# Attention block with a routed path: the first eleven stretches in another written order, and tanh, gate and product of the routed path at other places

## The chip, the cores and the metric

The kernel runs on one core of one Trainium2 chip. A core has five engines that work side by side, each through its own instructions in the order in which the program gives them: TensorE (PE, with its weight loads shown as PEld), VectorE (DVE), ScalarE (ACT), GpSimd (POOL) and SyncE (SP), which here only issues DMA transfers. An engine that waits for another one is told so by a semaphore, and what stands behind the waiting instruction on that engine waits too. The metric is the device time of one execution in microseconds (us), the median over several runs.

## The reference

The computation has two paths over the same 2048 rows of 640 features. `xn` is the layer norm of `x`.

```python
xn = layernorm(x)                                  # 2048 x 640
q  = xn @ wq                                       # 32 heads of 192
k, v = last 512 rows of the caches, per head
s  = concat_heads(softmax(q @ k.T * 192**-0.5) @ v) @ wo
r  = xn @ w_r                                      # routed path: the two rows with the largest r
y  = (silu(x_sel @ w_gate) * (x_sel @ w_up)) @ w_down * sigmoid(r_sel)
g  = silu(xn + scatter of y to those two rows)
out = x + s * g
```

Nearly all the arithmetic is in the first path: the query projection, the scores, the weighted values and the output projection.

## The kernel before

**Units, steps and stretches.** A unit is 128 query rows of one pair of heads; there are 256. A step is four units (512 rows, one pair of heads), and its query projection is three groups of five matmuls, one group for each 128 of the pair's 384 columns. Units are worked in 86 stretches: stretches 0 and 1 have two units each, all others three (unit n of 4 or more is in stretch 2 + (n-4)//3). What is done for a unit is spread over several stretches: its scores in one, its weighted values in the next, its share of the output projection some stretches later.

**Everything has a written place.** The program is emitted with a manual schedule: each engine's order is the order of the statements. Stretches 11 to 84 come from a function that writes the same order for each (`stretch`), the last from a list, and the first eleven (0 to 10, which also hold the layer norm and the first loads) from a list of tokens, `FIRST`, one line for each stretch after the opening line. A token is an operation and its numbers:

- `x.t.lo.hi` loads rows of x (SP's queue; `.a` at the end: ACT's queue); `k`, `v`, `wq`, `wo` load the other operands; `kT.p` transposes the keys of pair p by DMA on SP.
- `bn`, `as` take the layer norm's sums (on DVE, or on ACT with a short tail on POOL); `sq`, `rc`, `pw` form the scale; `ap.n.e` applies it to row block n on engine e (v DVE, a ACT, g POOL); `turn` and `xT` transpose the result, on PE or by DMA on SP.
- `q.i.c` is the projection group c of step i on PE, `qe` takes it out of PSUM, scaled (a `v` at the end: DVE; otherwise ACT, so also where numbers stand behind the letter, as in all of step 0, which is done in halves).
- `S.j` are the scores of stretch j on PE; `M.n.h` is the row maximum of unit n, head h on DVE; `E.n.h` the exponential on ACT; `P.n` the DMA transpose of the result on SP.
- `O.n` or `OO.n.m` are the weighted values on PE, `Oe` takes them out, divided by the sums (`R`, DVE); `T.j` is their DMA transpose; `W.w` is one block of the output projection on PE, `We` takes it out.
- `sx` and `ex` are tiny activations that bring in the tables of the square root and of the exponential; `B.j.s` runs what the rest of the program has put down for stretch j, slot s. Nothing is put down for a stretch before the twelfth, so the `B` tokens of the list issue nothing.

**PSUM.** Two banks (`ps_f`) serve the projection groups, single `O.n` and the transposes on PE; six (`ps_p`) serve the scores, `OO` and the output projection. A new tile gets the bank whose last reader stands earliest in the written order, and PE waits until that reader is done. The three groups of a step therefore need the first group to be out before the third can start.

**The routed path** rides in the slots of the stretches: `at(n, slot, f)` puts f into the stretch of unit n. In a stretch written by the function, slot 0 is directly behind the scores' matmuls, slot 1 behind the last exponential and its transpose, slot 2 behind the first output projection block and its way out, slot 3 at the very end. `m_mul` is a small gate-and-up product for 512 of 1536 columns (20 matmuls, a tanh, two operations on DVE, then `m_hT`, a DMA transpose). `m_tanh(n)` and `m_gate(n)` (ACT L627, DVE L630) turn row block n into the silu factor; the tanh's target is one of two buffers, by n even or odd, so a tanh must wait for the gate of two blocks before. The step from a stretch to the next on DVE is: values out, transposed, what stands in slot 3, then the next stretch's row maxima.

Of the kernel before, what the change touches and what calls it, by code (L numbers as in the profile page):

```python
# [21 lines left out]
def kernel(ctx, tc, A_x, A_k_cache, A_v_cache, A_wq, A_wo, B_x, B_w_r, B_w_gate, B_w_up, B_w_down, out):  # L22
    nc = tc.nc
    P = 128
    _, S, D = A_x.shape
# [3 lines left out]
    W = min(4096, max(256, Sk // 4))  # L29
# [45 lines left out]
    def f_tile(shape, dtype, name):  # L75
        return ps_f.tile(shape, dtype, name=name, tag="f")
# [358 lines left out]
    M = {}  # L435
# [119 lines left out]
    def m_ffn_piece(fb, q):  # L555
        def f():
            if q == 0:
                M["wgu"] = M["w"].tile([P, 2, DC, 512], BF16, name="wgu", tag="w")
            w, dc = divmod(q, DC)
            src = (B_w_gate, B_w_up)[w].rearrange("(c p) f -> p c f", p=P)  # L560
            nc.sync.dma_start(out=M["wgu"][:, w, dc, :], in_=src[:, dc, fb * 512:(fb + 1) * 512])
        return f

    def m_mul(fb):
        def f():
            gu = f_tile([P, 2, P], FP32, "gu_ps")
# [49 lines left out]
    def m_add(n):  # L616
        def f():
            nc.gpsimd.tensor_scalar(out=xn[:, n, :], in0=xn[:, n, :], scalar1=0.5, scalar2=0.0, op0=ALU.mult, op1=ALU.add)
            for j in range(2):
                yh = M["s"].tile([P, D], BF16, name="yh", tag="t1")  # L620
                nc.gpsimd.tensor_scalar(out=yh, in0=M["y_bc"][:, j, :], scalar1=M["oh"][:, n, j:j + 1], scalar2=0.0, op0=ALU.mult, op1=ALU.add)  # L621
                nc.gpsimd.tensor_tensor(out=xn[:, n, :], in0=xn[:, n, :], in1=yh, op=ALU.add)  # L622
        return f

    def m_tanh(n):
        M["z", n] = M["ws"[n % 2]].tile([P, D], FP32, name="tz", tag=("w", "t2")[n % 2])
        nc.scalar.activation(out=M["z", n], in_=xn[:, n, :], func=ACT.Tanh)  # L627

    def m_gate(n):
        nc.vector.scalar_tensor_tensor(out=xn[:, n, :], in0=M["z", n], scalar=1.0, in1=xn[:, n, :], op0=ALU.add, op1=ALU.mult)  # L630
# [128 lines left out]
    for fb, n0 in enumerate((72, 91, 106)):  # L759
        for q in range(2 * DC):  # L760
            at(n0 + q, 0, m_ffn_piece(fb, q))
        at(n0 + 14, 2, m_mul(fb))
        at(n0 + 14, 3, m_hT(fb))
    for q in range(FC // 2):
        at(121 + 2 * q, 0, m_wd_piece(q))
    at(124, 3, m_sig)
    at(138, 2, m_down)
    for n in range(NTB):
        at(147 + 2 * n, 3, m_add(n))
        at(186 + 2 * n, 1, lambda n=n: m_tanh(n))  # L770
        at(186 + 2 * n, 3, lambda n=n: m_gate(n))
    at(220, 3, fin_open)


# [5 lines left out]
    for j in range(2, NST):  # L780
        due = sum(st_of[4 * i] <= j + 1 for i, _ in todo)
        k = max(due, 2) if j % 4 != 1 else max(due, 3)
# [3 lines left out]
        k = 2 if len(ready) >= 2 and len(q_in[j]) <= 2 and (done + 1) <= 1.5 * (j - 4) else 1  # L786
        k = {NST - 4: 1, NST - 3: 1, NST - 2: 3, NST - 1: 2}.get(j, k)
# [69 lines left out]

    for token in FIRST:
# [43 lines left out]
```

## Time and profile before

| | |
|---|---|
| runs | 803.88 us median of 3 (802.24 to 804.67) |
| profiled execution | 803.23 us, span 801.5 us, granted TensorE clock 0.996 |
| busy in the span | PE 785.5, DVE 625.2, ACT 482.0, POOL 174.8 us |
| first 120 us | PE busy 111.6 us |
| 300 to 400 us | PE busy 100.0 us |
| last 61.5 us | PE busy 54.7 us |

The profile is of one execution. A row of the timeline gives the start in us from the span's first instruction, the time from the first start to the last end, the engine (SPq is SP's queue issuing a DMA), the line, the operation, output and inputs, and how many instructions are merged; in brackets stands idle time before it and what ended that. In the rows by windows the figures are, for each stretch of time, busy us of PE, PEld, DVE, ACT and POOL with their counts, the granted TensorE clock (1.00 is full), the DMA engines' mean share and GB/s. Durations of neighbours overlap: two exponentials that last 0.67 us each with a readout behind them start 0.66 us apart, so a step in a chain is taken from start to start.

### The profile page before, as it was taken

The page shows a single profiled execution, that of the slowest core. Times are in us where ns is not written, and L with a number is a line of the kernel's source. Part 1 is how long each engine was busy: PE and PEld are TensorE (multiplying, and loading weights), DVE is VectorE, ACT ScalarE, POOL GpSimd, SP SyncE. Part 2 cuts the span into 40 slices and gives each one's busy share as a digit, 9 for nine tenths or more (in the row PEclk, how much of TensorE's full clock was granted, in tenths as well). Part 3 has the DMA queues.
Part 4 walks back from the last instruction along what each step waited for, and adds up shares of the span by engine and source line. Part 5 has one row for each costly group of instructions (what it writes and reads, how often), then busy time and mean ns, then how long its engine had stood idle before and what let it go on. Part 6 is the DMA issues. An engine that isn't in the chain of part 4 may idle for free. (4 is left out here: it accounts for less than half of the span.)

```text
span 801.5 us, 15649 instructions
## 1 busy us (share of the span) xinstructions
PE 785.5 (98%) x5748; PEld 481.5 (60%) x5748; DVE 625.2 (78%) x1243; ACT 482.0 (60%) x1303; POOL 174.8 (22%) x194
## 2 busy tenths in 40 slices
PE   8899999999999999999999999999999999999996
PEld 4456556665666566666556665666566665566565
DVE  6876668989888777777777777777788887877786
ACT  7886676556655556655565556565566865565560
POOL 1330000000000000000001999920000000265954
PEclk9999999999999999999999999999999999999999
DMA  8999998789979999699997999879997889997994
GB/s 239 192 207 218 201 189 143 136 183 193 177 137 201 205 206 206 128 216 199 215 219 139 164 188 201 143 140 173 201 165 137 160 177 202 168 195 154 166 176 117
DMA packets 453389, 143.80 MB, mean 179 GB/s; under 512 B 422350, under 2 KB 452816, under 8 KB 453312
## 3 DMA queue, kind: packets, MB, share of 16 engines
q1 hardware_dynamic: 449872, 138.76, 92.8%
q0 software_dynamic: 928, 2.50, 1.1%
q10 hardware_dynamic: 2512, 1.54, 0.7%
q8 instruction: 45, 0.74, 0.4%
q14 instruction: 32, 0.26, 0.1%
HBM read 39.98 MB, written 2.62 MB: 53 GB/s over the span
## 5 line engine op out<-in xcount | busy, mean ns | idle before, releaser
L337 ACT ACTIVATE pexp<-sc,nm 128x512 bf16<-128x512 f32 x512 | 348.4, 696 | 292.5 <-issue 242.5
L330 DVE TENSOR_REDUCE nm<-sc 128x1 f32<-128x512 f32 x512 | 314.7, 681 | 78.7 <-PE sc L322 78.7
L301 PE MATMUL q_ps<-xnT,wq_p 128*128 128x512 bf16 (+1 forms) x975 | 226.3, 376 | 3.2 <-ACT pexp L337 0.8
L404 PE MATMUL w_ps<-wo_g,oT 128*128 128x320 bf16 x1542 | 223.2, 299 | 0.5 <-DMA oT<-o_sb 0.5
L404 PEld LDWEIGHTS <-oT 128*128 128x128 bf16 x1542 | 150.2, 98 | 71.0 <-DMA oT<-o_sb 0.8
L356 PE MATMUL o_ps<-v_sb,pT 128*128 128x192 bf16 x2048 | 185.2, 246 | 2.4 <-DMA pT<-pexp 1.3
L356 PEld LDWEIGHTS <-pT 128*128 128x128 bf16 x2048 | 170.9, 98 | 18.1 <-issue 4.9
L301 PEld LDWEIGHTS <-wq_p 128*128 128x128 bf16 x975 | 88.4, 98 | 127.1 <-issue 37.5
L371 DVE TENSOR_TENSOR o_sb<-o_ps,lsum 128x384 bf16<-128x384 f32 x239 | 131.6, 557 | 40.2 <-PE o_ps L356 22.0
L315 PE MATMUL sc<-kT,qT 128*128 128x512 bf16 x512 | 126.1, 382 | 0.9 <-DMA kT<-k_raw 0.9
L418 DVE TENSOR_TENSOR s_acc<-s_acc,w_ps 128x320 f32<-128x320 f32 x192 | 92.1, 483 | 32.2 <-PE w_ps L404 32.2
L337 ACT ACTIVATION_READ_ACCUMULATOR pexp<-sc,nm 128x1 f32 x512 | 109.8, 214 | 0.0
L293 ACT ACTIVATE qT<-q_ps 128x512 bf16<-128x512 f32 (+1 forms) x179 | 98.8, 606 | 1.3 <-PE q_ps L301 1.1
L315 PEld LDWEIGHTS <-qT 128*128 128x128 bf16 x512 | 49.0, 98 | 42.7 <-issue 2.1
L322 PE MATMUL sc<-kT,qT 64*128 64x512 bf16 x512 | 70.6, 382 | 0.0
L643 POOL TENSOR_TENSOR s_acc<-s_acc,xn 128x640 f32<-128x640 f32 x16 | 22.5, 1403 | 113.7 <-DVE s_acc L418 113.7
L322 PEld LDWEIGHTS <-qT 64*128 64x128 bf16 x512 | 18.1, 94 | 47.0 <-issue 36.8
L622 POOL TENSOR_TENSOR xn<-xn,yh 128x640 bf16<-128x640 bf16 x32 | 44.7, 1396 | 2.7
L612 POOL DMA_DIRECT2D y_d<-y_sb x4 | 2.2, 552 | 172.2 <-DVE y_sb L609 172.2
L644 POOL TENSOR_TENSOR s_acc<-s_acc,x_fin 128x640 f32<-128x640 f32 x16 | 22.4, 1400 | 62.5 <-DMA x_fin<-in_A_x_dram 61.5
L489 POOL DMA_DIRECT2D c_d<-cand x1 | 0.5, 547 | 155.4 <-DVE cand L487 155.4
L621 POOL TENSOR_SCALAR yh<-y_bc,oh 128x640 bf16<-128x640 bf16 x32 | 25.7, 803 | 5.0 <-DMA y_bc<-y_d 3.5
(105 smaller groups left out, 235.2 us busy)
## 6 DMA issues: line engine op xcount, KB each, us to landing
wo_g<-in_A_wo_dram SPq DMA_DIRECT2D x16, 480.0 KB, 4.4
wq_p<-in_A_wq_dram SPq DMA_DIRECT2D x14, 480.0 KB, 5.0
v_sb<-in_A_v_cache_dram SPq DMA_DIRECT2D x16, 384.0 KB, 4.0
k_raw<-in_A_k_cache_dram SPq DMA_DIRECT2D x30, 192.0 KB, 3.2
pT<-pexp SPq DMA_TRANSPOSE x256, 3.7
x_fin<-in_A_x_dram SPq DMA_DIRECT2D x16, 160.0 KB, 2.8
x_in<-in_A_x_dram SPq DMA_DIRECT2D x6, 320.0 KB, 4.8
wgu<-in_B_w_gate_dram SPq DMA_DIRECT2D x15, 128.0 KB, 2.8
```

Of the source, the lines that this page charges most:

```text
L293: nc.scalar.activation(out=out, in_=in_, func=ACT.Copy, scale=scale)
L301: nc.tensor.matmul(q_ps, lhsT=wq_of[g * PAIRS + pr][:, dc, c * P:(c + 1) * P], rhs=xnT[:, t5 * 4 + lo:t5 * 4 + hi, dc, :], start=(dc == 0) ...
L315: nc.tensor.matmul(sc_of[n][hh], lhsT=qT_of[i][:, 2 * hh, u * P:(u + 1) * P], rhs=kp[:, :, 2 * hh, :], start=True, stop=False)
L322: nc.tensor.matmul(sc_of[n][hh], lhsT=qT_of[i][hs, 1, u * P:(u + 1) * P], rhs=kp[hs, :, 1, :], start=False, stop=True)
L330: nc.vector.tensor_reduce(out=nm_of[j][:, c:c + 1], in_=sc_of[n][hh], axis=AX.X, op=ALU.max, negate=True)
L337: nc.scalar.activation(out=pe_of[n][:, hh, :], in_=sc_of[n][hh], func=ACT.Exp, bias=nm_of[j][:, c:c + 1], scale=1.0, accum_out=l_of[j][:, ...
L356: nc.tensor.matmul(ps[:, hh, :], lhsT=pT_of[n][:, hh, jj, :], rhs=v_sb[:, hh, jj, :], start=(jj == 0), stop=(jj == NJ - 1))
L371: nc.vector.tensor_tensor(out=osb_of[j][:, m], in0=ps, in1=l_of[j][:, 2 * m:2 * m + 2].unsqueeze(2).to_broadcast([P, 2, Dh]), op=ALU.mult)
L404: nc.tensor.matmul(w_ps, lhsT=oT_of[j][:, stretches[j].index(n), c % 3, :], rhs=wo_of[g][:, c, lo:hi], start=(c == 0), stop=(c == CPG - 1))
L418: nc.vector.tensor_tensor(out=acc, in0=acc, in1=w_ps, op=ALU.add)
L621: nc.gpsimd.tensor_scalar(out=yh, in0=M["y_bc"][:, j, :], scalar1=M["oh"][:, n, j:j + 1], scalar2=0.0, op0=ALU.mult, op1=ALU.add)
L622: nc.gpsimd.tensor_tensor(out=xn[:, n, :], in0=xn[:, n, :], in1=yh, op=ALU.add)
```

## The change

The list of the first eleven stretches is written in another order, with the same matmuls, scores and transfers. What differs beyond order: two row blocks (4 and 14) take their layer-norm sums on DVE instead of ACT; some ways out of PSUM and applications of the norm change engine; the loads `k.1.0`, `wq.1` and `wq.2` go from ACT's queue to SP's, the loads `x.0.3`, `k.2.1` and `k.3.0` to ACT's; the exponential's table comes in stretch 0 instead of ahead of it.

In the routed path the product for the first 512 columns moves from stretch 29, slot 2 to stretch 30, slot 3, the two others from slot 2 to slot 3 of their stretches (35 and 40). The tanh moves from slot 1 to slot 0, and the gate of an even block from slot 3 to slot 2; the gate of an odd block stays in slot 3.

```diff
     for fb, n0 in enumerate((72, 91, 106)):
         for q in range(2 * DC):
             at(n0 + q, 0, m_ffn_piece(fb, q))
-        at(n0 + 14, 2, m_mul(fb))
-        at(n0 + 14, 3, m_hT(fb))
+        at(n0 + (16, 14, 14)[fb], 3, m_mul(fb))
+        at(n0 + (16, 14, 14)[fb], 3, m_hT(fb))
...
         at(147 + 2 * n, 3, m_add(n))
-        at(186 + 2 * n, 1, lambda n=n: m_tanh(n))
-        at(186 + 2 * n, 3, lambda n=n: m_gate(n))
+        at(186 + 2 * n, 0, lambda n=n: m_tanh(n))
+        at(186 + 2 * n, 2 + n % 2, lambda n=n: m_gate(n))
...
     FIRST = """
-B.3.3 x.0.0.1.a x.0.1.2 k.0.0 bn.0.0 k.0.1.a bn.1.0 x.0.2.3 bn.0.1 sx sq.0.1 wq.0 bn.1.1 sq.1.2 kt.0.a rc.0.1 ap.0.v rc.1.2 kt.1.v x.0.3.4 ap.1.v bn.2.0 turn.0.a turn.1.v q.0.0.0.2 q.0.2.0.2 ex bn.2.1 qe.0.0.v.0.2 k.1.0.a bn.3.0 bn.3.1 qe.0.2.v.0.2 wq.1.a x.1.2.4 q.0.1.0.2 qe.0.1.a.0.2 x.1.0.2 pw.2.4 
-S.0 k.1.1 as.4 ap.2.v ap.3.v turn.2.v turn.3.a M.0.0 q.0.0.2.4 E.0.0 M.1.0 q.0.2.2.4 qe.0.0.v.2.4 E.1.0 bn.7.0 q.0.1.2.4 M.0.1 qe.0.2.v.2.4 v.1 qe.0.1.a.2.4 bn.6.0 B.2.0 bn.7.1 E.0.1 
-S.1 bn.6.1 x.2.0.2 M.1.1 q.1.2 x.2.2.4 as.5 q.1.0 pw.4.8 v.0 M.2.1 E.1.1 qe.1.2.a M.2.0 E.2.0 R.0 M.3.1 E.2.1 as.8 q.1.1 ap.6.g ap.4.v ap.5.v M.3.0 B.3.2 E.3.0 qe.1.0.v P.0 kT.1 bn.11.0 B.3.1 bn.9.0 ap.7.v O.0 qe.1.1.v E.3.1 bn.11.1 P.1 
-S.2 B.3.0 P.2 B.2.1 bn.9.1 xT.4.6 xT.6.8 M.4.0 as.10 P.3 B.4.0 M.5.0 pw.8.12 Oe.0.a M.4.1 O.1 E.5.0 M.5.1 q.2.0 E.5.1 x.3.0.2 Oe.1.v E.4.0 M.6.0 E.6.0 qe.2.0.v T.0 x.3.2.4 E.4.1 P.4 q.2.1 R.1 q.2.2 M.6.1 qe.2.1.v B.2.2 ap.8.g qe.2.2.v E.6.1 ap.9.g O.2 
-S.3 Oe.2.a ap.11.v M.7.0 P.5 M.8.0 M.8.1 as.12 ap.10.g O.3 E.7.0 Oe.3.a P.6 E.8.0 q.3.1 q.3.0 M.9.1 M.9.0 E.8.1 M.7.1 bn.13.0 E.7.1 qe.3.0.v OO.4.5 xT.8.10 R.2 E.9.0 Oe.4.v E.9.1 xT.10.12 qe.3.1.a Oe.5.v q.3.2 qe.3.2.v bn.13.1 P.8 
-S.4 T.1 O.6 as.15 B.2.3 q.4.1 B.7.2 P.7 Oe.6.a M.10.1 P.9 R.3 M.10.0 E.10.0 M.12.0 q.4.0 E.12.0 wo.0.0 M.11.0 wo.0.1 E.10.1 E.11.0 P.10 qe.4.1.v T.2 M.12.1 OO.7.8 M.11.1 E.12.1 qe.4.0.v E.11.1 O.9 Oe.7.v Oe.8.v Oe.9.v as.14 
-S.5 pw.12.16 P.11 q.4.2 M.13.0 E.13.0 M.13.1 P.12 M.14.0 M.14.1 M.15.0 E.14.0 ap.15.g B.5.3 B.4.3 E.14.1 q.5.0 qe.5.0.a E.13.1 M.15.1 qe.4.2.v W.0 B.6.3 ap.14.v E.15.0 OO.10.11 R.4 Oe.10.a E.15.1 T.3 B.5.2 Oe.11.a P.14 O.12 Oe.12.a ap.12.g P.13 We.0.v B.6.1 
-S.6 q.5.1 M.16.0 E.16.0 B.4.1 xT.14.16 B.8.0 B.5.0 P.15 ap.13.g M.17.1 M.16.1 M.17.0 qe.5.1.a B.7.3 xT.12.14 E.16.1 k.2.0 q.5.2 M.18.0 B.4.2 M.18.1 W.2 R.5 E.17.0 wo.1.0 E.18.0 We.2.v E.17.1 k.2.1 B.7.1 P.16 OO.13.14 E.18.1 W.1 q.6.0 B.6.2 qe.5.2.v P.18 Oe.13.a Oe.14.a We.1.v O.15 T.4 P.17 
-S.7 Oe.15.v qe.6.0.v M.20.0 q.6.1 B.10.3 M.19.0 M.21.0 qe.6.1.v E.19.0 B.5.1 M.21.1 M.20.1 M.19.1 E.20.0 q.6.2 E.21.0 E.19.1 E.20.1 W.3 O.18 W.4 T.5 wq.2.a v.2 qe.6.2.v E.21.1 We.4.v OO.16.17 k.3.0 R.6 We.3.a Oe.16.v Oe.17.a 
-S.8 M.22.0 Oe.18.a M.23.1 E.22.0 B.9.1 P.21 M.22.1 q.7.0 R.7 M.24.1 P.19 M.23.0 P.20 E.22.1 E.23.0 B.7.0 q.7.1 qe.7.0.a k.3.1 qe.7.1.a E.23.1 W.6 M.24.0 W.5 We.6.v E.24.0 wq.3 E.24.1 OO.19.20 B.6.0 P.22 Oe.19.a T.6 We.5.v Oe.20.a B.9.0 
-S.9 P.23 M.26.0 kT.3 B.10.1 M.26.1 O.21 Oe.21.v M.25.1 E.26.0 q.8.0 M.25.0 E.26.1 E.25.0 E.25.1 W.7 q.7.2 B.10.2 M.27.0 qe.8.0.a P.24 OO.22.23 E.27.0 M.27.1 qe.7.2.v E.27.1 T.7 P.26 R.8 B.8.1 Oe.22.v Oe.23.a q.8.1 P.25 kT.2 We.7.v 
-S.10 M.28.0 M.28.1 M.29.0 qe.8.1.a O.24 R.9 B.8.3 B.8.2 B.9.2 Oe.24.v P.27 E.28.0 v.3 M.30.0 E.28.1 q.9.0 qe.9.0.v E.29.0 M.30.1 E.30.0 OO.25.26 M.29.1 B.10.0 P.28 Oe.25.a q.8.2 E.29.1 B.9.3 E.30.1 O.27 qe.8.2.a Oe.26.a T.8 W.9 P.29 P.30 Oe.27.a W.8 wo.1.1 We.9.a T.9 We.8.a
+x.0.0.1.a x.0.1.2 bn.0.0 x.0.3.4.a bn.0.1 k.0.0 bn.1.0 B.2.0 x.0.2.3 k.0.1.a sq.0.1 wq.0 rc.0.1 sx B.3.3 bn.1.1 ap.0.v x.1.0.2 sq.1.2 rc.1.2 kt.0.a turn.0.a bn.3.0 kt.1.a bn.3.1 ap.1.v turn.1.v bn.2.0 bn.2.1 q.0.0.0.2 x.1.2.4 qe.0.0.v.0.2 q.0.2.0.2 q.0.1.0.2 v.0 qe.0.2.v.0.2 bn.4.0 qe.0.1.v.0.2 
+S.0 bn.4.1 pw.2.4 ex bn.6.0 ap.2.v k.1.0 ap.3.v M.0.0 turn.2.a turn.3.v M.0.1 q.0.0.2.4 wq.1 E.0.0 k.1.1 qe.0.0.v.2.4 q.0.2.2.4 bn.7.0 B.3.0 E.0.1 q.0.1.2.4 qe.0.2.v.2.4 x.2.2.4 bn.7.1 qe.0.1.v.2.4 bn.6.1 M.1.0 x.2.0.2 as.5 M.1.1 pw.4.8 
+S.1 B.3.1 M.2.0 q.1.2 M.3.0 B.4.0 qe.1.2.v M.2.1 v.1 q.1.1 kT.1 E.1.0 q.1.0 P.0 E.1.1 ap.4.v qe.1.1.a M.3.1 ap.6.v E.2.0 qe.1.0.v B.2.2 E.3.0 R.0 ap.5.g P.1 E.3.1 B.5.3 bn.9.0 O.0 ap.7.g E.2.1 as.8 bn.9.1 bn.11.0 Oe.0.v xT.4.6 
+S.2 M.4.0 M.6.0 bn.11.1 M.5.0 as.10 xT.6.8 P.2 E.5.0 O.1 P.3 Oe.1.v E.6.0 M.4.1 pw.8.12 q.2.0 E.4.0 M.5.1 B.3.2 B.5.2 qe.2.0.v q.2.2 x.3.0.2 x.3.2.4 E.4.1 ap.11.v E.5.1 T.0 M.6.1 P.4 qe.2.2.v R.1 q.2.1 qe.2.1.v ap.10.g bn.13.0 E.6.1 P.6 
+S.3 R.2 M.7.0 as.12 O.2 E.7.0 M.8.0 Oe.2.v ap.8.a M.7.1 O.3 Oe.3.v E.7.1 P.5 q.3.1 qe.3.1.a M.8.1 E.8.0 ap.9.g M.9.1 B.4.3 E.8.1 xT.10.12 M.9.0 T.1 q.3.0 E.9.0 q.3.2 OO.4.5 qe.3.0.v E.9.1 qe.3.2.v Oe.4.a as.15 R.3 Oe.5.v 
+S.4 O.6 xT.8.10 P.8 bn.13.1 M.10.0 P.7 Oe.6.a M.11.0 q.4.1 M.12.0 M.10.1 qe.4.1.v B.2.3 P.9 wo.0.0 E.11.0 bn.14.0 bn.14.1 E.12.0 wo.0.1 M.11.1 E.10.0 T.2 E.10.1 B.7.2 E.11.1 M.12.1 E.12.1 OO.7.8 Oe.7.v O.9 P.11 P.10 P.12 Oe.8.v Oe.9.v 
+S.5 q.4.0 pw.12.16 M.14.0 M.13.0 qe.4.0.a ap.15.v R.4 M.13.1 M.15.0 B.2.1 M.14.1 q.5.0 E.13.0 ap.14.g B.6.2 B.6.1 M.15.1 E.13.1 q.4.2 E.14.0 qe.5.0.v W.0 E.14.1 B.10.3 E.15.0 We.0.v OO.10.11 ap.13.g Oe.10.a Oe.11.a qe.4.2.v xT.14.16 E.15.1 
+S.6 R.5 T.3 B.6.3 O.12 M.16.0 M.17.0 B.4.1 P.14 ap.12.a q.5.1 Oe.12.v B.7.3 M.17.1 P.13 E.16.0 M.16.1 E.17.0 M.18.1 E.16.1 W.2 B.8.0 qe.5.1.a xT.12.14 M.18.0 E.18.0 P.15 E.18.1 T.4 We.2.v q.5.2 E.17.1 OO.13.14 qe.5.2.v P.16 k.2.0 B.7.1 P.18 Oe.13.v Oe.14.v q.6.0 W.1 B.5.0 O.15 We.1.a qe.6.0.a 
+S.7 M.21.0 P.17 Oe.15.a E.21.0 M.19.1 M.19.0 T.5 E.19.0 M.20.0 M.21.1 v.2 q.6.1 B.10.2 wo.1.0 qe.6.1.v k.2.1.a M.20.1 k.3.0.a E.19.1 B.4.2 q.6.2 E.21.1 R.6 E.20.0 W.4 P.21 We.4.a O.18 E.20.1 OO.16.17 Oe.16.v wq.2 P.19 W.3 qe.6.2.v We.3.a Oe.17.v 
+S.8 M.22.0 q.7.1 P.20 k.3.1 Oe.18.a M.24.0 E.22.0 M.23.0 M.23.1 M.22.1 E.23.0 q.7.0 E.22.1 E.23.1 W.6 qe.7.0.a M.24.1 W.5 E.24.0 B.9.0 E.24.1 OO.19.20 B.8.1 wq.3 P.23 We.6.v R.7 We.5.a Oe.19.v Oe.20.v B.9.1 P.22 B.5.1 B.10.0 
+S.9 B.6.0 qe.7.1.a O.21 M.26.0 Oe.21.v M.26.1 q.8.0 E.26.0 M.25.1 q.7.2 M.25.0 E.26.1 E.25.0 qe.7.2.v E.25.1 M.27.1 M.27.0 E.27.0 W.7 E.27.1 qe.8.0.a We.7.v R.8 P.24 OO.22.23 T.6 q.8.1 Oe.22.a Oe.23.v 
+S.10 M.28.1 qe.8.1.a M.28.0 E.28.0 M.29.0 q.9.0 B.7.0 kT.2 P.25 M.29.1 O.24 B.8.3 P.26 B.8.2 P.27 M.30.0 E.28.1 R.9 qe.9.0.v Oe.24.a OO.25.26 T.7 E.29.0 E.29.1 M.30.1 B.9.3 T.8 O.27 q.8.2 P.28 Oe.25.a v.3 wo.1.1 E.30.0 W.8 E.30.1 B.10.1 B.9.2 We.8.a Oe.26.v P.30 P.29 Oe.27.a T.9 qe.8.2.a W.9 kT.3 We.9.a
```

## The prediction

> **What bounds the kernel now.** I read the page first, then PE's busy time by windows, then what PE waited for.
>
> ```profile
> span 801.5 us, 15649 instructions
> ...
> 0.00:120.00 120.00, 111.62 (x750) 63.10 (x751) 85.02 (x176) 87.62 (x237) 16.22 (x46) 0.99 1.04 208
> 300.00:400.00 100.00, 100.00 (x760) 61.86 (x757) 74.92 (x150) 57.14 (x158) 0.00 (x0) 1.00 1.03 193
> ```
>
> In the middle PE is never idle (100.00 of 100), so there only PE's own work and hidden stalls between its matmuls count. In the first 120 us it is idle 8.4 us, and here the written order changes. PE's waits in that part, the longest and one that comes up below:
>
> ```profile
> PE o_ps L356 <- DVE qT L291: 1.0, 1, 1.0
> ...
> PE q_ps L301 <- DMA xnT<-xn: 0.4, 1, 0.4
> ```
>
> All are single waits of at most 1 us. What this list doesn't show is PE's clock, here by single microseconds (the figure ahead of the last two):
>
> ```profile
> 22.00:23.00 1.00, 0.67 (x8) 0.67 (x8) 1.00 (x4) 0.97 (x4) 0.75 (x2) 1.00 2.16 126
> 23.00:24.00 1.00, 0.15 (x2) 0.00 (x1) 1.00 (x3) 1.00 (x4) 0.32 (x1) 1.00 0.27 41
> 24.00:25.00 1.00, 0.94 (x3) 0.40 (x3) 0.97 (x4) 1.00 (x4) 0.00 (x0) 0.57 1.28 287
> 27.00:28.00 1.00, 1.00 (x8) 0.31 (x5) 0.68 (x2) 0.00 (x0) 0.78 (x3) 0.73 1.15 158
> ```
>
> After two thin microseconds (1.2 idle) the clock is near half from 24 to about 27.5, so stretch 2's scores run slowly. The timeline of that time, which gives the pace of ACT, DVE and SP and PE's places:
>
> ```profile
> 8.31 1.28 ACT L241 ACT_TABLE_LOAD   x1
> 15.85 0.67 ACT L293 ACTIVATE qT<-q_ps 128x256 bf16<-128x256 f32 x2
> 17.35 1.83 DVE L330 TENSOR_REDUCE nm<-sc 128x1 f32<-128x512 f32 x3
> 18.69 1.52 SPq L119 DMA_TRANSPOSE kT<-k_raw  x1
> 20.30 3.39 SPq L342 DMA_TRANSPOSE pT<-pexp  x2
> 21.23 0.74 ACT L233 ACTIVATE junk_a<-x_in 128x640 bf16<-128x640 bf16 x1
> 22.92 0.67 ACT L337 ACTIVATE pexp<-sc,nm 128x512 bf16<-128x512 f32 x1
> 23.78 3.06 SPq L262 DMA_TRANSPOSE xnT<-xn  x2
> 24.06 2.68 PE L315 MATMUL sc<-kT,qT 128*128 128x512 bf16 x6 [0.91 <-DMA kT<-k_raw]
> 27.84 0.83 PE L356 MATMUL o_ps<-v_sb,pT 128*128 128x192 bf16 x8
> 29.48 3.40 PE L301 MATMUL q_ps<-xnT,wq_p 128*128 128x512 bf16 x15 [0.80 <-ACT pexp L337]
> ```
>
> **The change, step by step.** It is counted against the profiled execution, 803.23 us; the runs' median, 803.88, lies 0.65 above that. "Lead" is how much sooner PE stands at the same work.
>
> *Up to stretch 1: nothing.* The first loads come about as early. k.0.1 is now issued behind x.0.3, but the keys' transposes on PE have the norm of blocks 0 and 1 as cover, which still ends last ahead of the first projection. The exponential's table (1.28) leaves an idle stretch of ACT for the place where `as.4` stood (an `as` is 1.69: from 21.23 to the exponential at 22.92). I take 0; the bounds are minus and plus 0.4, the difference of the two.
>
> *Stretch 2's scores: lead 2.2.* Before, they wait for kT.1, issued at 18.69 behind the transpose of unit 0, until 24.06. Now kT.1 stands directly behind the load v.1, and both its halves are loaded early, so it is in time. Last is then the third projection group's way out on DVE. DVE turns to stretch 1's maxima at 17.35, and from there stand 4 maxima (0.61 each, a third of 1.83), 2 applications (0.4 each) and 2 ways out (0.6 each, near a maximum): 4.4, so 21.8. The lead is 24.06 - 21.8 = 2.2. `as.5` on ACT now stands ahead of E.1.0 and feeds the applications; if that is late, up to 1.0 of this is lost.
>
> *The half clock and xn: lead 2.8.* A stretch's scores take 2.15 at full clock (41.04 to 43.19 below), here 27.84 - 24.06 = 3.78. The 1.6 go with the thin microseconds: now PE works to 20.6 and then has unit 0's values and the scores with under 1 us of idle between. That would be a lead of 3.8, but step 2's projection waits for xn's second transpose. (Its row names an exponential; the two transposes issued from 23.78 fit better.) In the new order that pair follows the transpose of unit 1, which needs E.1.1: 15.85 + 0.6 for the last ways out, `as.5` 1.69, two exponentials of 0.67, so 19.5, and 1.5 for SP to issue: 21.0 instead of 23.78. The lead is 2.8, and by their rows ACT and DVE keep it to stretch 4.
>
> ```profile
> 41.04 1.46 PE L315 MATMUL sc<-kT,qT 128*128 128x512 bf16 x6
> 43.19 0.83 PE L356 MATMUL o_ps<-v_sb,pT 128*128 128x192 bf16 x8
> 43.86 2.32 PE L301 MATMUL q_ps<-xnT,wq_p 128*128 128x512 bf16 x10
> 46.97 2.15 PE L356 MATMUL o_ps<-v_sb,pT 128*128 128x192 bf16 x24 [0.79 <-DMA pT<-pexp]
> 51.10 2.33 PE L301 MATMUL q_ps<-xnT,wq_p 128*128 128x512 bf16 x10
> 53.27 0.57 PE L404 MATMUL w_ps<-wo_g,oT 128*128 128x320 bf16 x3
> 54.35 1.40 PE L404 MATMUL w_ps<-wo_g,oT 128*128 128x320 bf16 x9 [0.51 <-DMA oT<-o_sb]
> ```
>
> *Stretch 4, SP's queue: lead 1.7.* SP issues nearly without a pause here:
>
> ```profile
> 28.55 0.57 SPq L100 DMA_DIRECT2D x_in<-in_A_x_dram  x1
> 30.33 1.22 SPq L377 DMA_TRANSPOSE oT<-o_sb  x1
> 31.60 0.57 SPq L100 DMA_DIRECT2D x_in<-in_A_x_dram  x1
> 32.65 4.39 SPq L342 DMA_TRANSPOSE pT<-pexp  x3
> 37.13 2.97 SPq L262 DMA_TRANSPOSE xnT<-xn  x2
> 43.06 3.29 SPq L342 DMA_TRANSPOSE pT<-pexp  x2
> ```
>
> A transpose costs it (37.13 - 32.65)/3 = 1.49. That of unit 7, issued at 43.06, releases the values at 46.97. From xn's first transpose to it stand 11 transposes and 2 loads before, and 12 and 2 after (the transpose of unit 2 now comes behind xn): 1.5 lost. Two waits of SP (29.12 to 30.33 and 32.17 to 32.65, together 1.7) fill, as the values and exponentials that they waited for come sooner. So the lead of 2.8 holds: values at 44.1. But one group of step 4 (1.08, half of 53.27 - 51.10), which stood ahead of these values and filled PE meanwhile, now comes in stretch 5 and is still owed: 2.8 - 1.1 = 1.7. SP's pace bounds this: 12 transposes at 1.22 (30.33) would give 3.2 more, at 1.65 (half of 3.29) take 1.9.
>
> *Stretches 5 to 10: lead 2.2.* W.0 stops waiting for its transposed values (+0.5), as the owed group stands ahead of it. The wait for xn's last blocks goes (+0.4). In stretch 6 the sixth score tile takes the bank that E.15.1 reads, now written behind the ways out of units 10 and 11 on ACT: -0.4. The two loads on ACT's queue in stretch 7 hold up E.19.1, but W.4's banks are those of E.21.0 and E.19.0: 0. The other exchanges on PE cost nothing, being equal work. Lead at stretch 11: 1.7 + 0.5 + 0.4 - 0.4 = 2.2. All its unknowns bound it by 0 and 3.8.
>
> *Routed path: 0.7.* Two gates at the head of a stretch hold up its maxima, and with three projection groups that reaches PE:
>
> ```profile
> 597.63 1.46 PE L315 MATMUL sc<-kT,qT 128*128 128x512 bf16 x6
> 598.31 1.55 DVE L630 SCALAR_TENSOR_TENSOR xn<-tz,xn 128x640 bf16<-128x640 f32 x2
> 600.49 0.69 ACT L337 ACTIVATE pexp<-sc,nm 128x512 bf16<-128x512 f32 x1 [3.48 <-DVE nm L330]
> 601.95 1.79 PE L404 MATMUL w_ps<-wo_g,oT 128*128 128x320 bf16 x12
> 603.16 1.09 ACT L293 ACTIVATE qT<-q_ps 128x512 bf16<-128x512 f32 x2
> 603.82 1.24 PE L301 MATMUL q_ps<-xnT,wq_p 128*128 128x512 bf16 x5
> 605.44 0.78 ACT L627 ACTIVATE tz<-xn 128x640 f32<-128x640 bf16 x1
> ```
>
> The third group needs the first one's way out, 603.16 + 0.6, and starts at 603.82; the product ahead of it ends at 601.95 + 1.79 less the tail of 0.16 by which such rows overlap the next (51.10 + 2.33 against 53.27): 603.58. So 0.24 is lost. Stretches 69 and 73 also have three groups behind two gates. With the even gate in slot 2 one is left at the head (0.75 less), so 3 x 0.24 = 0.7 goes. In slot 0 a tanh can wait for the odd gate of the stretch before, which ends about 1.5 into the stretch; 0.78 for a tanh gives 2.3, ahead of the first exponential (2.86 here, about 2.6 without the second gate). So the tanh is hidden by 0.3; without that cover it would cost 0.3 at each of these stretches. The moved products are the same 20 matmuls between other neighbours: 0, with bounds of minus and plus 0.3.
>
> Sum: 803.23 - 2.2 - 0.7 = 800.3. I add half of the median's 0.65 over its profile, since one execution is no rule: 800.6.
>
> A page bears on the clock's row. The Trainium skill, "TensorE: Matmul & The Clock Gate", section "HAM oscillation — how this bites in real kernels", says to avoid idle gaps of PE of more than about 3.4 us. Here the longest wait is 1.0 us and the clock halved all the same, so the row decides against that figure; by the page alone nothing would have halved, and the sum would lack the 1.6 in stretch 2, part of which stretch 4 takes back in any case.
>
> **Rivals.** *The half clock comes back ahead of stretch 4's values.* PE ends the one group of step 4 at 43.86 + 1.08 - 2.8 = 42.1 and waits to 44.1: 2.0 of idle, more than the 1.2 before 24. Whether it halves the clock depends on what stands around it. It would cost the same 1.6: 802.2.
>
> *The lead doesn't reach stretch 11.* DVE and ACT are busy nearly throughout from 22 to 25 in the rows above, and any operation that is late there gives the lead back. Then the gates' 0.7 alone stays: 803.23 - 0.7 + 0.3 = 802.8.
>
> *Slower, by SP.* If a transpose costs 1.70 (half of 3.39) instead of 1.49, 12 of them lose 2.5, the owed group 1.1, and the longer wait halves the clock (1.6): 2.8 - 2.5 - 1.1 - 1.6 = -2.4, and with the +0.5 and +0.4 of stretches 5 and 6 not coming and the -0.4 staying -2.8: 803.23 + 2.8 - 0.7 + 0.3 = 805.6. It decides from 1.63 on, where the lead of 1.7 at stretch 5 is gone. For it speaks that the queue is full in both orders; against it, that 1.49 is what three in a row took.
>
> **How the numbers follow.** Forecast 0.5, clock 0.2, no lead 0.15, SP 0.15. The forecast's own range is 799.0 to 801.8. Faster by over 0.3% (about what a measurement of this kernel can tell from no change) is below 801.5: most of the forecast and a quarter of the clock's, 0.53. Slower by over 0.3% is above 806.3, SP's worse part with sums that I have not seen: 0.12. The same: 0.35. The range holds the first three cases: 798.8 to 804.4.
>
> **What would show it.** Right: stretch 2's scores start near 22 at full clock, xn's second transpose lands near 26.6, stretch 4's values start near 44 and still behind a transpose, the third group of stretches 65, 69 and 73 follows without a pause, and stretch 11 starts 2.2 sooner. Wrong: the clock halves before 50, SP's transposes take over 1.6, or stretch 2 starts after 23.

## The result

The changed kernel takes 802.49 us, median of 22 runs (800.55 to 805.18), against 804.96 (802.24 to 807.58, 22 runs) for the kernel before on the same chip: a ratio of 0.9973, 95% interval 0.9963 to 0.9983. Forecast were 800.6 us and a step of 3.3 us down from 803.88; measured were 2.5. The time lies outside the forecast's own range (799.0 to 801.8), between the 802.2 and the 802.8 of two rivals. In two later groups of runs the same kernel gave 0.9972 (0.9954 to 0.9991) and 0.9998 (0.9985 to 1.0011): its own median hardly moves (802.84 and 803.00), that of the kernel before does (805.2 and 803.13). So the measured gain lies between nothing and 2.5 us, by the group of runs.

The page and PE's busy time by windows, for the changed kernel (profiled execution 804.91 us):

```profile
span 803.1 us, 15627 instructions
...
0.00:120.00 120.00, 109.91 (x738) 64.11 (x739) 83.64 (x176) 82.68 (x219) 15.41 (x43) 0.96 1.03 203
300.00:400.00 100.00, 100.00 (x758) 61.86 (x755) 75.88 (x147) 58.22 (x160) 0.00 (x0) 1.00 1.02 192
```

The middle is as before. In the first 120 us PE is idle 10.1 us, not 8.4, and the clock is 0.96, not 0.99: there the change has lost something. PE's waits in these 120 us name it:

```profile
PE tp_k L273 <- DMA k_raw<-in_A_k_cache_dram: 3.2, 2, 2.0
PE o_ps L356 <- ACT pexp L337: 2.0, 1, 2.0
```

The first row was not in the list of before: PE waits 3.2 us for the first keys, in the part where I had put nothing. PE's timeline at the places that the prediction names, for the changed kernel:

```profile
6.08 0.23 PE L273 MATMUL tp_k<-ident,k_raw 128*128 128x128 bf16 x1 [1.26 <-DMA k_raw<-in_A_k_cache_dram]
8.29 0.71 PE L273 MATMUL tp_k<-ident,k_raw 128*128 128x128 bf16 x5 [1.98 <-DMA k_raw<-in_A_k_cache_dram]
...
11.39 3.10 PE L301 MATMUL q_ps<-xnT,wq_p 128*128 128x256 bf16 x15 [0.68 <-DVE xnT L259]
14.32 1.03 PE L315 MATMUL sc<-kT,qT 128*128 128x512 bf16 x4
...
25.11 1.53 PE L315 MATMUL sc<-kT,qT 128*128 128x512 bf16 x6 [0.47 <-DVE qT L291]
...
29.51 2.66 PE L301 MATMUL q_ps<-xnT,wq_p 128*128 128x512 bf16 x11 [1.35 <-DVE nm L330]
...
47.51 3.39 PE L356 MATMUL o_ps<-v_sb,pT 128*128 128x192 bf16 x24 [1.96 <-ACT pexp L337]
...
109.37 1.46 PE L315 MATMUL sc<-kT,qT 128*128 128x512 bf16 x6
```

and the same places in the kernel before that the prediction has not shown:

```profile
5.90 1.39 PE L273 MATMUL tp_k<-ident,k_raw 128*128 128x128 bf16 x12 [0.26 <-DVE stats L163]
...
9.41 1.89 PE L301 MATMUL q_ps<-xnT,wq_p 128*128 128x256 bf16 x15 [0.67 <-DVE xnT L259]
11.13 1.03 PE L315 MATMUL sc<-kT,qT 128*128 128x512 bf16 x4
...
107.15 1.46 PE L315 MATMUL sc<-kT,qT 128*128 128x512 bf16 x6
```

Stretch 0 starts 3.2 us later (14.32 against 11.13). From there the new list makes up ground: stretch 2's scores are 1.0 late, step 2's projection stands level (29.51 and 29.48). The start is late because of the first loads. DMA issues of the first 2.4 us, with the KB of each and the median us from issue to landing (SP's two loads of x, nearly the same in both, are left out), first before, then changed:

```profile
k_raw<-in_A_k_cache_dram ACTq DMA_DIRECT2D x1, 192.0 KB, 4.5
k_raw<-in_A_k_cache_dram SPq DMA_DIRECT2D x1, 192.0 KB, 4.7
x_in<-in_A_x_dram ACTq DMA_DIRECT2D x1, 160.0 KB, 3.2
```

```profile
x_in<-in_A_x_dram ACTq DMA_DIRECT2D x2, 160.0 KB, 3.3
k_raw<-in_A_k_cache_dram SPq DMA_DIRECT2D x1, 192.0 KB, 4.8
k_raw<-in_A_k_cache_dram ACTq DMA_DIRECT2D x1, 192.0 KB, 6.6
```

ACT's queue now carries `x.0.3` ahead of the second key half. That half is issued 0.5 us later (1.68 against 1.20) and then takes 6.6 us instead of 4.5: it is there at 8.3, not 5.7. Behind it stand 21 transposes on PE and, as the row at 11.39 shows, a clock that has fallen: the fifteen matmuls take 3.10 us, not 1.89, and the granted clock is 0.50 from 8 to 14. The Trainium skill, "DMA: Bandwidth & Descriptors", section "Rules for kernel authors", says that DMAs issued by SP and ACT run on the same 16 DMA engines and interleave. These rows don't test that, since the late half stands on the load's own queue; `e_kfirst` below agrees in its one profile, where the load on ACT's queue goes with a later key half on SP's (7.2 against 5.9 us).

### The profile page after: what moved, and what is told of

It is laid out like the page before. It is cut to its first block, busy times and chain, and to the rows that moved or that the text cites. A ratio compares the mean times of both kernels' runs of the same rounds, so it can differ in the third digit from the quotient of the medians.

```text
span 803.1 us, 15627 instructions
## 1 busy us (share of the span) xinstructions
PE 785.6 (98%) x5748; PEld 483.7 (60%) x5748; DVE 625.9 (78%) x1247; ACT 480.5 (60%) x1291; POOL 174.5 (22%) x191
## 5 line engine op out<-in xcount | busy, mean ns | idle before, releaser
L371 DVE TENSOR_TENSOR o_sb<-o_ps,lsum 128x384 bf16<-128x384 f32 x246 | 135.8, 557 | 42.4 <-PE o_ps L356 23.0
```

The lines of the kernel that those rows point to most:

```text
L371: nc.vector.tensor_tensor(out=osb_of[j][:, m], in0=ps, in1=l_of[j][:, 2 * m:2 * m + 2].unsqueeze(2).to_broadcast([P, 2, Dh]), op=ALU.mult)
```

## The experiments

The theory after these traces: the place of one load, `x.0.3`, cost what the list had gained; the other steps held. Rivals: the half clock ahead of stretch 4's values did it; the lead is absorbed by DVE and SP ahead of stretch 11 whatever the start; the routed path brought less than thought. Each group of runs shares a chip and runs of the kernel before. Lists are broken into lines of my own in the diffs.

**The changed kernel again, and the keys ahead of the load.** `e_again` is the changed kernel; `e_kfirst` issues both key halves ahead of `x.0.3`:

```diff
 x.0.0.1.a x.0.1.2 bn.0.0
-x.0.3.4.a bn.0.1 k.0.0 bn.1.0 B.2.0 x.0.2.3 k.0.1.a sq.0.1 wq.0
+k.0.0 k.0.1.a x.0.3.4.a bn.0.1 bn.1.0 B.2.0 x.0.2.3 sq.0.1 wq.0
```

> The changed kernel once more, for a second profile of it and for times on the same chip as its variants. The time: ratio 0.997. If the half clock at the start (7.4 to 14) and in stretch 4 (48 to 51.4) of the first profile belongs to the order, this profile shows both again; if it hangs on where the clock's window happens to lie, one of them is missing here and the places of stretches shift by up to 1.6 us.

> The changed kernel with one exchange on ACT's queue: the second half of the first keys (k.0.1) is issued ahead of the row block x.0.3 again. In the changed kernel's profile k.0.1 lands at 8.24 us (before: 5.66) and stretch 0's scores start at 14.32 (before: 11.13). If the late keys are what the first eleven stretches lost (theory: late keys), k.0.1 lands near 5.9, the scores of stretch 0 start near 11.2, and the time is 2 to 3.2 us under the changed kernel's, a ratio to the kernel before of 0.993 to 0.995. If later waits (SP's queue, ways out on DVE) take up a late start anyway (rival: absorbed), the time stays at the changed kernel's ratio of 0.997.

Measured: 0.9972 (0.9954 to 0.9991) again, and 0.9954 (0.9936 to 0.9973) with the keys first. In the second the half on ACT's queue lands at 5.0, but now the one on SP's queue is late, at 7.2; `x.0.3` is still issued early, 0.65 us behind it:

```profile
7.24 0.82 PE L273 MATMUL tp_k<-ident,k_raw 128*128 128x128 bf16 x6 [1.60 <-DMA k_raw<-in_A_k_cache_dram]
...
10.44 3.24 PE L301 MATMUL q_ps<-xnT,wq_p 128*128 128x256 bf16 x15 [0.68 <-DVE xnT L259]
```

So one microsecond of the two came back at the keys (8.29 became 7.24) and the projection still ran at half pace; the medians are 0.7 us apart (802.84 and 802.16), and the intervals overlap. It points at the load, and doesn't settle it.

**More warm-up matmuls.** `e_warm` fills the wait for the keys:

```diff
-    for _ in range(10):
+    for _ in range(24):
```

> The changed kernel with 24 instead of 10 warm-up matmuls on an idle tile, so that PE is at work to about 8 us while it would wait for the keys. It leaves the loads as they are. If part of the loss at the start is PE's clock (0.50 from 7.4 to 14 in the changed kernel's profile), the clock stays at 1.00 there, the first projection takes 1.9 instead of 3.1 us, and the time falls by about 1.2 us, a ratio of 0.9958. If the clock at the start is not typical of the runs or is absorbed later, the ratio stays at 0.997.

Measured: 0.9968 (0.9954 to 0.9982), no faster than the changed kernel (803.35 against 802.84). In its profile the projection ran at full pace and stretch 0 started at 12.9, but only 0.7 of 1.2 us was left at stretch 11 (108.40 against 109.13 in `e_again`). The 24 matmuls lasted to 9.3, though the keys were there at 7.9, so they held up the keys' transposes (9.12) by 1.2 us: this run doesn't separate the clock from the keys.

**The load, in both directions.** `e_x03sp` is the changed kernel with the load on SP's queue behind `wq.0`; block 3's sums follow it:

```diff
-x.0.0.1.a x.0.1.2 bn.0.0 x.0.3.4.a bn.0.1 k.0.0 bn.1.0 B.2.0 x.0.2.3 k.0.1.a sq.0.1 wq.0 rc.0.1
+x.0.0.1.a x.0.1.2 bn.0.0 bn.0.1 k.0.0 bn.1.0 B.2.0 x.0.2.3 k.0.1.a sq.0.1 wq.0 x.0.3.4 rc.0.1
...
-turn.0.a bn.3.0 kt.1.a bn.3.1 ap.1.v
+turn.0.a kt.1.a ap.1.v
...
-q.0.2.0.2 q.0.1.0.2 v.0
+q.0.2.0.2 bn.3.0 bn.3.1 q.0.1.0.2 v.0
```

`e_bx03` is the kernel before with only this load moved:

```diff
-k.0.0 bn.0.0 k.0.1.a bn.1.0
+k.0.0 bn.0.0 x.0.3.4.a k.0.1.a bn.1.0
...
-rc.1.2 kt.1.v x.0.3.4 ap.1.v
+rc.1.2 kt.1.v ap.1.v
```

> The changed kernel with the load x.0.3 back on SP's queue behind wq.0, so that the second key half is the second load on ACT's queue again, as in the kernel before; the sums of block 3 (bn.3) follow two places later on DVE. If the late key half is what cost the lead, it lands near 5.9 instead of 8.24, the first projection starts near 9.4 instead of 11.4 at full pace, stretch 0's scores near 11.3 instead of 14.3, and the time falls 2 to 3 us under the changed kernel: 0.994 of the kernel before, or less. If stretches 4 to 10 are bound by something else than PE's start (SP's transposes, DVE), stretch 0 is as early but stretch 11 stays near 109 and the ratio near 0.997.

> The kernel before with the one load x.0.3 moved from SP's queue behind wq.0 to ACT's queue ahead of the second key half. If the place of this load is the cause, the key half lands near 8.2 instead of 5.85, the first projection starts 2 us later, near 11.4, stretch 0's scores 2 to 3 us later, and what of it reaches the end shows in the time: up to 2 to 3 us more, 1.003. If the old list has slack for it, for it waits at 24 for a key transpose by DMA anyway, stretch 2 stands near 24 again and the ratio is 1.000.

Measured: 0.9939 (0.9925 to 0.9954), 798.70 us of 5 runs, with the load put back; 1.0052 (1.0036 to 1.0069), 807.96 us of 6 runs, with it moved in the old list, against 803.25 for the kernel before. The second moves nothing but the load. The first also moves block 3's sums; in the changed kernel these stand on DVE ahead of block 1's norm, which is done at 8.20, and PE goes on with the keys at 8.29, so in that profile the sums cost nothing. The old list has no slack for the load; PE's timeline of `e_bx03` shows the same two waits, 3.4 us in all:

```profile
6.73 0.29 PE L273 MATMUL tp_k<-ident,k_raw 128*128 128x128 bf16 x1 [1.08 <-DMA k_raw<-in_A_k_cache_dram]
9.31 1.35 PE L273 MATMUL tp_k<-ident,k_raw 128*128 128x128 bf16 x11 [2.29 <-DMA k_raw<-in_A_k_cache_dram]
...
13.06 3.36 PE L301 MATMUL q_ps<-xnT,wq_p 128*128 128x256 bf16 x15 [0.68 <-DVE xnT L259]
16.21 1.05 PE L315 MATMUL sc<-kT,qT 128*128 128x512 bf16 x3
```

Both directions were then put beside each other on one chip: `e_x03sp2` is the same kernel as `e_x03sp`, `e_after2` the changed kernel.

> The changed kernel with x.0.3 back on SP's queue, again, now beside the changed kernel and two variants on one chip. If the place of this load is what cost the gain, it is 0.994 of the kernel before here too, about 3 us under the changed kernel; if the first figure was of few executions, it is nearer the 0.9975 of the variant whose key half went out on DVE.

> The changed kernel itself, on the same chip, as what the three beside it are to be compared with. Expected 0.997 of the kernel before, with the late key half (landing 8.2 to 8.5) and the start of stretch 0's scores at 14.1 to 14.3.

Measured: 799.06 us (798.43 to 800.67, 10 runs; 0.9952, 0.9935 to 0.9968) and 803.00 us (801.29 to 804.09, 12 runs; 0.9998). The ranges don't meet; 3.9 us lie between the medians, for one load and the two sums that follow it. The timeline of `e_x03sp2` (profiled execution 798.76):

```profile
6.25 0.51 PE L273 MATMUL tp_k<-ident,k_raw 128*128 128x128 bf16 x6 [0.91 <-DMA k_raw<-in_A_k_cache_dram]
...
8.44 1.90 PE L301 MATMUL q_ps<-xnT,wq_p 128*128 128x256 bf16 x15 [0.79 <-DMA wq_p<-in_A_wq_dram]
10.18 1.03 PE L315 MATMUL sc<-kT,qT 128*128 128x512 bf16 x4
...
22.46 1.46 PE L315 MATMUL sc<-kT,qT 128*128 128x512 bf16 x6
...
26.16 2.35 PE L301 MATMUL q_ps<-xnT,wq_p 128*128 128x512 bf16 x10 [0.73 <-DMA xnT<-xn]
...
44.21 2.15 PE L356 MATMUL o_ps<-v_sb,pT 128*128 128x192 bf16 x24 [1.83 <-ACT pexp L337]
...
104.64 1.46 PE L315 MATMUL sc<-kT,qT 128*128 128x512 bf16 x6
```

The 4.1 us at stretch 0 (14.32 - 10.18) are three terms: the keys 2.0 (8.29 - 6.25), the transposes behind them 0.9 (11.39 - 8.29 against 8.44 - 6.25) and the projection 1.2 (14.32 - 11.39 against 10.18 - 8.44). The last two are matmuls at half pace, and that is not bound to the late keys alone. In all six profiles with the load ahead of the key half and ten warm-up matmuls the fifteen matmuls take 2.59 to 3.36 us, but so they do in three of the nine with it behind `wq.0` (3.21 to 3.33; the other six 1.88 to 1.90). One of the three is `e_x03sp` (profiled execution 801.25, the slowest of its five):

```profile
9.05 3.33 PE L301 MATMUL q_ps<-xnT,wq_p 128*128 128x256 bf16 x15 [1.27 <-ACT kT L274]
12.22 1.03 PE L315 MATMUL sc<-kT,qT 128*128 128x512 bf16 x4
```

Against it 2.1 us are left at stretch 0 (14.32 - 12.22). So the place of the load is shown as the cause by the times of both directions; how much of it is the wait, and how much a clock that would have fallen in some executions anyway, is not.

**Stretch 4's gap.** `e_q40` puts `q.4.0` back behind `q.4.1`; `e_x03q` and `e_x03q2` do this on top of `e_x03sp`:

```diff
-P.7 Oe.6.a M.11.0 q.4.1 M.12.0
+P.7 Oe.6.a M.11.0 q.4.1 q.4.0 M.12.0
...
-S.5 q.4.0 pw.12.16
+S.5 pw.12.16
```

> The changed kernel with the projection group q.4.0 moved back from the head of stretch 5 into stretch 4, right behind q.4.1. If the 2.0 us of idle PE ahead of the values of units 7 and 8 halve the clock, the group fills 1.08 of it, the clock stays full from 48 to 52, stretch 4 takes about 8 instead of 9.24 and the time falls 1.1 to 2.4 us under the changed kernel: 0.994 to 0.996 of the kernel before. If the half clock comes from what lies around the gap, or the time is given back by stretch 11, the ratio stays near 0.997.

> Both edits of the two runs before in one kernel: x.0.3 back on SP's queue behind wq.0, and q.4.0 back in stretch 4. If the two losses are separate, the gains add: 3 to 5 us under the changed kernel, 0.991 to 0.993 of the kernel before, stretch 11 near 105. If both give way to one chain behind them, it is no better than the better of the two.

> x.0.3 back on SP's queue and q.4.0 back in stretch 4, again. If the group's place is worth nothing, as the run with it alone suggests, the time is that of the run with x.0.3 alone, within 0.001; if it saves the half clock of stretch 4, it is 1 to 1.6 us under it.

Measured: 0.9989 (0.9974 to 1.0004), 0.9953 (0.9936 to 0.9970) and 0.9956 (0.9940 to 0.9972). In all three profiles the clock is full from 48 to 52; by its ratio none is faster than the kernel without this edit (0.9972 and 0.9998, 0.9939, 0.9952). My expectation that it would save 1.1 to 2.4 us was wrong.

**The change in two halves.** `e_routed` is the kernel before with the places of tanh, gate and product alone, `e_list` with the list alone, `e_bagain` the kernel before once more.

```diff
-        at(n0 + 14, 2, m_mul(fb))
+        at(n0 + (16, 14, 14)[fb], 3, m_mul(fb))
...
-        at(186 + 2 * n, 1, lambda n=n: m_tanh(n))
-        at(186 + 2 * n, 3, lambda n=n: m_gate(n))
+        at(186 + 2 * n, 0, lambda n=n: m_tanh(n))
+        at(186 + 2 * n, 2 + n % 2, lambda n=n: m_gate(n))
```

> The kernel before with the routed path's places alone (tanh, gate, product). Theory as predicted: the pauses of 0.24 us ahead of the third group in stretches 65, 69 and 73 go, 0.7 us, a ratio of 0.9991, and the rest of the gain is the first eleven stretches'. Rival: the places carry most of the gain of 2.5 us, ratio 0.997.

> The kernel before with the new list alone (tanh, gate and product at their old places), the complement of the run with the routed path's places alone. If the two parts add, as their places far apart say, the list alone is 0.9990 to 0.9985 of the kernel before (the whole change 0.9973 less the 0.7 to 1.5 us of the routed path), the start is late again (first projection near 11.4), stretches 65, 69 and 73 take 9.24 again and stretches 11 to 84 together about 0.7 us more than with the new places. If the list did the whole, it is 0.997.

> The kernel before once more, for a second profile of it. If the half clock at 24 to 27.5 belongs to this order, it is there again, with stretch 2's scores at 24 or later; if the profile that the sum was made against was a lucky execution, stretch 11 starts 1 to 3 us later than its 107.15. The ratio is 1.000.

Measured: the routed path alone 0.9974 (0.9956 to 0.9993), the list alone 1.0003 (0.9984 to 1.0022), the kernel before 1.0002 (0.9982 to 1.0022). The list, with its late start, is worth nothing by itself. What the routed path is worth is read better from the trace, by PE's timeline of stretch 65, first with the list alone (old places), then in the changed kernel:

```profile
598.82 1.46 PE L315 MATMUL sc<-kT,qT 128*128 128x512 bf16 x6
...
603.13 1.79 PE L404 MATMUL w_ps<-wo_g,oT 128*128 128x320 bf16 x12
605.00 1.24 PE L301 MATMUL q_ps<-xnT,wq_p 128*128 128x512 bf16 x5
```

```profile
599.94 1.46 PE L315 MATMUL sc<-kT,qT 128*128 128x512 bf16 x6
...
604.25 1.79 PE L404 MATMUL w_ps<-wo_g,oT 128*128 128x320 bf16 x12
605.88 1.24 PE L301 MATMUL q_ps<-xnT,wq_p 128*128 128x512 bf16 x5
...
608.94 0.38 PE L315 MATMUL sc<-kT,qT 128*128 128x512 bf16 x1
```

With the old places the third group follows 1.87 us behind the start of the output projection, with the new ones 1.63: the 0.24 is gone, and the stretch takes 9.00 us (608.94 - 599.94). The same holds in stretches 69 and, but for 0.1, 73, in every profile with the new places. From stretch 11's scores to the end of the span the four profiles with the old places take 693.5 to 694.4 us, mean 694.0, and the thirteen with the new ones 692.4 to 695.3, mean 693.2: 0.8 between the means.

**Two ways to hold the clock at the start.** `e_x03v` takes the second key half out of PSUM on DVE in `e_x03sp`; `e_x03w` gives that kernel 14 warm-up matmuls.

```diff
-turn.0.a kt.1.a ap.1.v
+turn.0.a kt.1.v ap.1.v
```

```diff
-    for _ in range(10):
+    for _ in range(14):
```

> The changed kernel with x.0.3 back on SP's queue, as in the run before, and the second half of the first keys taken out of PSUM by DVE, not ACT (as in the kernel before). If the 1.27 us that PE waits ahead of the first projection, and the half clock behind it, still cost there, the wait is about 0.7, the three groups take 1.9 instead of 3.1 and the time falls by up to 1.2 us under that run: 0.9925. If that is absorbed by stretch 11, as it was with more warm-up matmuls, it stays at 0.994.

> x.0.3 back on SP's queue, and 14 warm-up matmuls ahead of the keys' transposes in place of 10, which fill PE's idle time of 0.8 us up to the landing of the keys. If the half clock in the first projection (9 to 12.9 in the profile) is what separates 798.5 us from 801.2 us among the executions, the projection runs at full pace, stretch 0's scores start near 10.5 to 11 instead of 12.2 and nearly all executions stand near 798.5, 0.994 or less. If that time is absorbed, it is the same as without them; if the four matmuls hold the keys up, up to 0.6 us more.

Measured: 0.9975 (0.9956 to 0.9993) and 0.9967 (0.9953 to 0.9981), both with a smaller gain than `e_x03sp` and `e_x03sp2` (0.9939 and 0.9952), though their intervals overlap that of the second. On DVE the key half stands ahead of block 1's norm, so PE waits for that norm instead, and the projection starts later and at half pace:

```profile
8.76 0.45 PE L258 MATMUL tp<-ident,xn 128*128 128x128 bf16 x5 [1.01 <-DVE xn L251]
9.89 3.21 PE L301 MATMUL q_ps<-xnT,wq_p 128*128 128x256 bf16 x15 [0.68 <-DVE xnT L259]
```

The 14 matmuls ran at half pace to the end, 7.25, and held up keys that were there at 6.23:

```profile
1.20 6.05 PE L138 MATMUL warm_ps<-idle 128*128 128x512 bf16 x14 [1.20 <-DVE idle L135]
```

The projection behind them did run at full pace (1.88) and stretch 0 started at 10.86, as expected; all the same the median is 800.72 us, against 799.06 for `e_x03sp2` on the same chip. Why, no run shows.

The version that beats both kernels is the changed one with `x.0.3` on SP's queue: 0.9952 and 0.9939 of the kernel before, about 4 us under the changed kernel on one chip.

## Why the prediction was wrong

| us | before | forecast | changed | load put back |
|---|---|---|---|---|
| stretch 0's scores | 11.13 | 11.1 | 14.32 | 10.18 |
| stretch 2's scores | 24.06 | 21.8 | 25.11 | 22.46 |
| step 2's projection | 29.48 | 26.6 | 29.51 | 26.16 |
| stretch 4's values | 46.97 | 44.1 | 47.51 | 44.21 |
| stretch 11's scores | 107.15 | 104.95 | 109.37 | 104.64 |
| profiled execution | 803.23 | 800.3 | 804.91 | 798.76 |

(Forecast: the column before less the step's lead; stretch 0 stood at nothing. Each other column is one profile, the last that of `e_x03sp2`.)

*Up to stretch 1: nothing.* This step failed. It said that the first loads come about as early, and that the norm of blocks 0 and 1 covers a later `k.0.1`. The key half landed 2.6 us later (8.3 against 5.7) and the norm covered nothing of it: on PE the first six of the keys' transposes stand ahead of those of the norm, and from the second on they need the late half. So everything behind them moved, and in this execution the clock had fallen. The bounds of minus and plus 0.4 came from ACT's table load and never touched a load's place in its queue. The cost was 3.2 us at stretch 0 against the profile of before, and 3.9 between the medians on one chip.

That is more than the miss. With the load put back the kernel gains 4.1 and 4.6 us (799.06 against 803.13, 798.70 against 803.25), where 3.3 were forecast. That its 0.9952 is near the forecast's 0.9959 (800.6 to 803.88) is in part luck: 0.95 us of it is an earlier start, 10.18 against 11.13, which I hadn't counted.

*Stretch 2's scores*, *the half clock and xn*, *stretch 4, SP's queue*, *stretches 5 to 10*: right in sign. With the load put back the four places stand at 22.46, 26.16, 44.21 and 104.64 in `e_x03sp2`, within 0.7 us of the forecast, but 0.8 to 1.9 later than it in `e_x03sp` (23.01, 27.41, 45.12 and 106.84). Taken from each kernel's own stretch 0, the leads over the kernel before are 2.1, 3.2, 2.7 and 1.0 us in the changed kernel and 0.7, 2.4, 1.8 and 1.6 in `e_x03sp2`, against 2.2, 2.8, 2.8 and 2.2 in the forecast (for the first: 24.06 - 11.13 less 25.11 - 14.32 is 2.1). So in the changed kernel the lead is there up to stretch 4's values, and the half clock takes 1.2 of it there (3.39 against 2.15); in `e_x03sp2` it is 1.5 short at stretch 2 and 1.0 at the values. Behind the values it falls by 1.7 with that 1.2, and by 0.2, where the forecast had 0.6 (2.8 to 2.2): stretches 5 to 10 came no worse than reckoned. At stretch 11 it is 0.6 to 1.2 short in all. That the list gains behind its start doesn't hang on these two profiles: from stretch 0's scores to stretch 11's it takes 93.8 to 95.5 us in thirteen profiles, the old one 96.0 to 98.7 in four. In the changed kernel all of it is spent on the late start.

*The half clock* of stretch 2, counted at 1.6 us, is not in every execution. The second profile of the kernel before has none there, with scores at full pace, and has one in the first projection in its place. The profile of `e_routed`, whose first eleven stretches are those of the kernel before, has it at stretch 2 again. First the one, then the other:

```profile
9.35 3.28 PE L301 MATMUL q_ps<-xnT,wq_p 128*128 128x256 bf16 x15 [0.68 <-DVE xnT L259]
...
25.45 1.46 PE L315 MATMUL sc<-kT,qT 128*128 128x512 bf16 x6 [0.79 <-DMA kT<-k_raw]
...
108.41 1.46 PE L315 MATMUL sc<-kT,qT 128*128 128x512 bf16 x6
```

```profile
24.30 2.54 PE L315 MATMUL sc<-kT,qT 128*128 128x512 bf16 x6 [0.92 <-DMA kT<-k_raw]
...
110.05 1.46 PE L315 MATMUL sc<-kT,qT 128*128 128x512 bf16 x6
```

They reach stretch 11 1.3 and 2.9 us later than the profile I summed against. That is a second, smaller flaw: adding half of 0.65 for it was too little, and it flattered the kernel before, not the change.

*Routed path: 0.7.* The mechanism and its 0.24 at each stretch were as said, and the tanh stayed hidden. The product moved 0.76 us from stretch 29 to stretch 30 and cost nothing in sum (9.77 and 9.55 became 9.00 and 10.31). The run of this half alone gave 2.1 us with 0.6 to 3.5 as its interval, which holds 0.7 just so; the 0.8 between the means from stretch 11 on lies nearer to 0.7 than to 2.1.

*The rivals.* That the half clock comes back ahead of stretch 4's values came true in this execution (the values' 24 matmuls took 3.39 us against 2.15), and its 802.2 is near what was measured, for another reason: the profiles of `e_after2` and `e_list` have no half clock there and reach stretch 11 at 108.5, so it is worth 0.6 to 0.9 us at most, and `e_q40` found no gain in removing its gap. The lead that doesn't reach stretch 11 comes nearest to what happened; not DVE or ACT took it between 22 and 25, but the first 8 us. SP's queue did not slow down: from xn's first transpose (24.28) to unit 7's (43.38) the changed kernel's twelve took 1.49 us each, less the 1.2 of the two loads. Two of the prediction's own signs of being wrong came: stretch 2 started after 23 (25.11), and the clock halved before 50.

## What to carry to other kernels

When a load moves to another queue, look at what now stands behind it there, and follow that transfer to the engine that waits for it; at the start of a kernel, where nothing else can run, a load's place can be worth more than what its bytes take (here 3.9 us, with the two sums, against 0.5: an estimate from 160 KB at 309 GB/s, the rate from 5 to 6 us in the changed kernel's profile). "Covered by other work" must be read in the order of the engine that waits: cover behind the waiting instruction is none. A term that rests on a short spell of half clock needs a second profile of the same kernel before it is counted.

## What was not expected of the hardware

With a load of 160 KB ahead of it on ACT's queue the key half took 6.0 to 7.6 us from issue to landing in seven profiles, and without it 3.4 to 4.9 in nine. With the keys first on both queues and the load behind, the half on SP's queue took 6.0, against 4.7 to 5.4 in those nine, but this is one profile. Why it is so much more than its share of the bytes no run shows.

The half clock comes and goes between executions of one order. The same list had it in the first projection in one profile (`e_x03sp`, 3.33 us for the fifteen matmuls) and not in the other (`e_x03sp2`, 1.90), and with stretch 4's values after a wait of 2.12 us in the first, but not after one of 1.83 in the second. The windows of these two profiles, from 47 to 49:

```profile
47.00:48.00 1.00, 1.00 (x8) 0.89 (x7) 0.34 (x1) 0.88 (x4) 1.00 (x2) 0.50 1.02 364
48.00:49.00 1.00, 1.00 (x4) 0.29 (x2) 0.56 (x1) 0.00 (x0) 1.00 (x2) 0.50 1.00 326
```

```profile
47.00:48.00 1.00, 1.00 (x8) 0.31 (x7) 0.00 (x0) 0.00 (x0) 1.00 (x2) 1.00 1.02 339
48.00:49.00 1.00, 1.00 (x7) 0.31 (x4) 0.77 (x2) 0.00 (x0) 0.99 (x4) 1.00 1.20 265
```

The Trainium skill, "TensorE: Matmul & The Clock Gate", section "What's actually happening", says that the clock is set by an activity window that runs freely, without regard to the kernel's start, and that a kernel's cold spell so varies from run to run. That fits these profiles; the gap of more than 3.4 us, which the prediction cited from the Trainium skill, was needed in none of them.
